# The channel MLP's first layer of an attention, gated-mixer and token/channel-mixer kernel: seven block products in place of eight, tokens in two parts

## The chip, the cores and the metric

One core of one Trainium2 chip runs the kernel. The metric is device time in microseconds (us). TensorE (PE) does the matrix products, VectorE (DVE), ScalarE (ACT) and GpSimd (POOL) the elementwise work, and SyncE (SP) issues the DMAs. Every engine takes its own instructions in a fixed order and waits on the others by semaphores.

## The reference

Three stages in a row, on 4 batches of 448 tokens with 768 channels. All weights come as 64-bit floats.

```python
def _attn_ref(q, k, v, g_q, g_k):            # 12 heads of 64
    q_n, k_n = rmsnorm(q, g_q), rmsnorm(k, g_k)
    attn = softmax(q_n @ k_n.T / sqrt(64))
    return attn @ v

def _moe_ref(x, w_in, w_spatial, b_spatial, w_out):
    h = np.maximum(x @ w_in, 0.0)
    u, v = h[..., :512], h[..., 512:]
    v_n = layernorm(v)
    v_s = np.einsum('ts,bsd->btd', w_spatial, v_n) + b_spatial[None, :, None]
    return (u * v_s) @ w_out

def _moe2_ref(x, w_tok1, w_tok2, w_ch1, w_ch2):
    xt = x.transpose(0, 2, 1)
    h = np.maximum(xt @ w_tok1, 0.0) @ w_tok2
    u = x + h.transpose(0, 2, 1)
    h2 = np.maximum(u @ w_ch1, 0.0) @ w_ch2  # 768 -> 1536 -> 768, the channel MLP
    return u + h2
```

## The kernel before, in words

Nearly every product is done at close to fp32 accuracy with three passes over values split in two (HI, rounded to fp32r, and LO, the rest): HI*HI, HI*LO and LO*HI (PASSES). A split is one ScalarE copy for HI and one subtraction for LO. A weight that comes as 64 bits is first made into an fp32 word by `convert`: one ScalarE Abs, two VectorE tensor_scalar and two VectorE scalar_tensor_tensor.

The program builds a list of operations and does not issue them as it writes them. `Plan.issue` gives each operation a cost and a time to be visible elsewhere (`estimate`), runs a forward and a backward list schedule eight times (`place`), keeps the shortest, and issues every engine's instructions in the order of its start times. The order on each engine is therefore static on the chip, and it follows from those estimates and from the buffers: a pool tag with `bufs` buffers makes its next tile wait for all users of the one that many tiles before. A `fence` opens a new pool where older ones lay, after all their users. PSUM has eight banks, in three kinds ("sc", "tp", "mm"). Nearly all instructions have line 405, where the planned calls are made, so this text goes by tiles.

The stages: attention per pair of heads, merged with the preparation of weights (`prepare_v`, `prepare_uo`, `prepare_next`) and with the gated mixer `moe` of the batches that are done; `moe` of the last batch beside the first steps of the token MLP (`first_tokens`); the token MLP (`Tokens`, tiles h1ps, u_ps); the channel MLP (`channels`, tiles h2ps, o_ps).

In `Tokens`, `sums` leaves u in fp32 tiles x, `store` writes them to the scratch u_d, and `turn` transposes each x tile and splits it into `ut`: 96 transposes on TensorE, 24 copies on ScalarE and 24 subtractions on VectorE of 128x448.

In `channels` (pools `keep`, `wp`, `cp`) the hidden layer has 12 blocks f of 128, taken in pairs. For each pair and each of four token blocks (512, 512, 512, 256), `up` makes two products of 18 matmuls (6 blocks of channels, 3 passes) into h2ps, with Relu and split out of PSUM, and then `down` of the block before adds its part of the second layer into `acc`: per 128 tokens two halves of 12 matmuls of 384 columns and one VectorE add. The weights of f = 0 and 1 come split from scratch (c1_d, c2_d, made in `prepare_next`); those of the ten others are loaded as 64 bits, converted and split in the stage itself, 40 times 128x384, with the subtraction on GpSimd. The tiles c1 and c2 have three buffers each.

Of the kernel before, what the change touches and what calls it, by code (L numbers as in the profile page):

```python
# [21 lines left out]
HI, LO = 0, 1  # L22
# [127 lines left out]
class Plan:  # L150
# [63 lines left out]
    def estimate(self, engine, fn, out, ins, kwargs):  # L214
# [29 lines left out]
        return max(475, shape[0] * n * 4 / 260), 2000  # L244
# [192 lines left out]
def attention_moe_mixer(  # L437
# [95 lines left out]
    c1_d = [scratch([P, 2, KD, P], F32R, f"c1_d{f}") for f in range(2)]  # L533
    c2_d = [scratch([P, 2, DM], F32R, f"c2_d{f}") for f in range(2)]
# [345 lines left out]
    def prepare_next(mp):  # L880
# [25 lines left out]
        n = NX // P  # L906
        for f in range(2):
            for j in range(0, KD, n):
                piece(
                    wdram(w_ch1)[j * P:(j + n) * P, f * P * W:(f + 1) * P * W].rearrange(  # L910
                        "(j p) f -> p j f", p=P), P, (n, P), c1_d[f][:, :, j:j + n])
                yield
        for f in range(2):
            for t in range(0, DM, NX):
                piece(wdram(w_ch2)[f * P:(f + 1) * P, t * W:(t + NX) * W], P, (NX,), c2_d[f][:, :, t:t + NX])
                yield

# [94 lines left out]
    class Tokens:  # L1012
# [75 lines left out]
        def turn(self, b, n, ut):  # L1088
            for j in range(n * KD // 2, (n + 1) * KD // 2):

                tp = psum.tile([P, C * P], "tp", "tp")
                for c, (t, m) in enumerate(TOK):
                    nc.tensor.transpose(tp[:, t:t + P], self.x[b, c][:, j * P:(j + 1) * P], ident)
                tpf = tp[:, :S]
                bs = slice(b * S, (b + 1) * S)
                nc.scalar.activation(ut[j][:, HI, bs], tpf, AF.Copy)
                nc.vector.tensor_tensor(
                    ut[j][:, LO, bs], tpf, ut[j][:, HI, bs].bitcast(F32), op=ALU.subtract)
                yield

# [5 lines left out]
    def channels(wp, cp, ut):  # L1106
        blocks = [(t0, min(512, NTOK - t0)) for t0 in range(0, NTOK, 512)]
        out_f = out.rearrange("b s d -> (b s) d")
        G = 2
        c1, c2 = {}, {}  # L1110
        N = DM // 2

        def load_up(f):
            t = wp.tile([P, 2, KD, P], F32R, tag="c1", bufs=3, name="c1")
            c1[f] = t
            if f < 2:
                nc.sync.dma_start(out=t.bitcast(F32), in_=c1_d[f].bitcast(F32))
                return
            for i in range(2):
                js = slice(i * KD // 2, (i + 1) * KD // 2)  # L1120
                raw = weights(
                    wp, "s", 2,
                    wdram(w_ch1)[i * N:(i + 1) * N, f * P * W:(f + 1) * P * W].rearrange(
                        "(j p) f -> p j f", p=P),
                    P, (KD // 2, P))
                convert(wp, "word", 1, raw, P, N, t[:, HI, js], t[:, LO, js], (KD // 2, P))

        def load_down(f):
            t = wp.tile([P, 2, DM], F32R, tag="c2", bufs=3, name="c2")
            c2[f] = t  # L1130
            if f < 2:
                nc.sync.dma_start(out=t.bitcast(F32), in_=c2_d[f].bitcast(F32))
                return
            for i in range(2):
                ns = slice(i * N, (i + 1) * N)
                raw = weights(
                    wp, "s", 2, wdram(w_ch2)[f * P:(f + 1) * P, i * N * W:(i + 1) * N * W], P, (N,))
                convert(wp, "word", 1, raw, P, N, t[:, HI, ns], t[:, LO, ns])
# [43 lines left out]
        for f0 in range(0, KC, G):  # L1182
            for nb, blk in enumerate(blocks):
                for f in range(f0, f0 + G):
                    for _ in up(f, blk):
                        pass
# [118 lines left out]
```

## Time and profile before

| | |
|---|---|
| median of 3 runs | 956.19 us (954.49 to 959.67) |
| the profiled execution | 952.84 us |
| its span, first to last instruction | 951.1 us |
| TensorE busy | 915.1 us (96%) |
| VectorE busy | 567.9 us (60%) |
| ScalarE busy | 452.1 us (48%) |
| GpSimd busy | 370.1 us (39%) |
| mean granted TensorE clock | 0.996 |

The busy share is a mean over stages. The channel MLP takes the last 350 us or so. TensorE's matmuls are pipelined: one that the profile gives 337 ns follows its neighbour after about half of that, so the pace of a run of them is read from the chain of work that ended last, which gives a stretch and a count.

### The profile page before, as it was taken

The numbers are of one execution on the slowest core, as the hardware profiler recorded it, in microseconds if no ns is written. First come the engines' busy times: TensorE is split into PE (matmuls) and PEld (weight loads), VectorE is DVE, ScalarE is ACT, GpSimd is POOL, SyncE is SP. The second block draws the span as 40 slices with busy tenths as digits, with TensorE's granted clock in tenths as the row PEclk, the third lists the DMA queues.
The fourth block names the chain that finished last, engine by engine and source line by source line (L and its number), as shares of the span: only waits on it lengthen the run. The fifth ranks groups of instructions, "written<-read, shape, count | busy, mean of one in ns | idle before, by whom it ended". The sixth has DMA issues, their size and how long they took to land.

```text
span 951.1 us, 15484 instructions
## 1 busy us (share of the span) xinstructions
PE 915.1 (96%) x5328; PEld 736.9 (77%) x5328; DVE 567.9 (60%) x1254; ACT 452.1 (48%) x1135; POOL 370.1 (39%) x538
## 2 busy tenths in 40 slices
PE   3898999999999999999999999999999999999998
PEld 1344366668767777677889999899898998999898
DVE  4787878775776767764151367534665556555434
ACT  5887877777676777765342345301312213122100
POOL 3767766785666664654124123101201102011100
PEclk9998999999999999999999999999999999999999
DMA  6544465666534565332673475721211212111024
GB/s 153 138 101 134 116 172 149 158 188 184 163 92 107 172 207 179 97 98 99 220 223 129 142 246 181 266 85 34 78 56 36 64 34 83 50 51 50 17 89 144
DMA packets 124654, 118.58 MB, mean 125 GB/s; under 512 B 74784, under 2 KB 108128, under 8 KB 123040
## 3 DMA queue, kind: packets, MB, share of 16 engines
q1 hardware_dynamic: 124576, 117.59, 41.0%
q8 instruction: 42, 0.69, 0.3%
q14 instruction: 36, 0.29, 0.1%
HBM read 89.77 MB, written 27.79 MB: 124 GB/s over the span
## 4 chain that ended last, share of the span: by engine, by line
PE 82%; ACT 5%; DVE 5%; DMA 3%; issue 2%; POOL 2%; SPq 1%; ACTq 0%; POOLq 0%; DVEq 0%
PE o_ps L405 18%; PE h2ps L405 18%; PE tp L405 9%; PE av L405 6%; PE xps L405 6%; PE ups L405 6%; PE sc L405 6%; PE sps L405 4%; PE u_ps L405 3%; PE h1ps L405 3%; PE vps L405 3%; ACT e L405 2%; DVE nm L405 1%; SPq L405 1%; DMA x<-x_d 1%
## 5 line engine op out<-in xcount | busy, mean ns | idle before, releaser
L405 PE MATMUL o_ps<-c,h 128*128 128x384 f32 x1008 | 179.7, 337 | 0.0
L405 PE MATMUL h2ps<-ut,c 128*128 128x512 f32 (+1 forms) x864 | 178.9, 364 | 0.0
L405 PEld LDWEIGHTS o_ps<-c,h 128*128 128x128 f32 x1008 | 175.0, 188 | 2.0 <-DVE acc L405 0.5
L405 PEld LDWEIGHTS h2ps<-ut,c 128*128 128x128 f32 x864 | 148.1, 189 | 24.3
L405 POOL TENSOR_SCALAR e<-e,sums 112x448 f32<-112x448 f32 x192 | 122.8, 656 | 63.0 <-DVE sums L405 35.1
L405 POOL TENSOR_TENSOR c<-word,c 128x384 fp32r<-128x384 f32 x40 | 40.5, 1014 | 265.1 <-ACT c L405 241.7
L405 ACT ACTIVATE e<-sc,nm 112x448 f32<-112x448 f32 x192 | 120.0, 637 | 29.1 <-PE tp L405 15.0
L405 DVE TENSOR_REDUCE nm<-sc 112x1 f32<-112x448 f32 x192 | 110.0, 614 | 22.3 <-PE sc L405 22.0
L405 PEld LDWEIGHTS tp<-ident,e 112*128 112x128 f32 x672 | 75.3, 142 | 47.0 <-POOL e L405 16.6
L405 PE MATMUL tp<-ident,e 112*128 112x112 f32 x672 | 101.9, 267 | 6.4 <-POOL e L405 3.2
L405 DVE TENSOR_TENSOR acc<-o_ps,acc 128x384 f32<-128x384 f32 x140 | 77.2, 555 | 29.6 <-PE o_ps L405 28.9
L405 ACT ACTIVATE h<-h2ps 128x512 fp32r<-128x512 f32 (+1 forms) x48 | 25.8, 538 | 116.5 <-PE h2ps L405 114.9
L405 ACT ACTIVATE c<-word 128x384 fp32r<-128x384 f32 x40 | 21.0, 525 | 123.0 <-DVE word L405 58.2
L405 DVE SCALAR_TENSOR_TENSOR h<-h2ps,h 128x512 fp32r<-128x512 f32 (+1 forms) x48 | 29.9, 624 | 82.3 <-ACT h L405 82.2
L405 ACT ACTIVATE et<-tp 128x448 f32<-128x448 f32 x120 | 63.4, 544 | 20.5 <-PE tp L405 19.9
L405 PE MATMUL ups<-xp,wu 128*128 128x448 f32 x288 | 69.6, 379 | 1.4 <-ACT vr L405 0.7
L405 PE MATMUL av<-et,v 128*64 128x448 f32 x288 | 67.4, 563 | 0.0
L405 PE MATMUL xps<-wo,g 128*128 128x256 f32 x432 | 63.3, 291 | 0.1
L405 PEld LDWEIGHTS xps<-wo,g 128*128 128x128 f32 x432 | 55.1, 190 | 5.0 <-issue 2.3
L405 PEld LDWEIGHTS ups<-xp,wu 128*128 128x128 f32 x288 | 51.7, 189 | 8.6 <-ACT vr L405 1.1
L405 DVE TENSOR_SCALAR word<-word 128x384 f32<-128x384 f32 (+1 forms) x92 | 34.2, 372 | 37.1 <-ACT word L405 35.7
L405 PE MATMUL vps<-wv,xp 128*128 128x512 f32 x216 | 55.1, 402 | 0.0
(105 smaller groups left out, 1414.5 us busy)
## 6 DMA issues: line engine op xcount, KB each, us to landing
raw<-in_moe_w_ch_dram SPq DMA_DIRECT2D x40, 384.0 KB, 3.2
wu<-wu_d SPq DMA_DIRECT2D x16, 768.0 KB, 5.1
wo<-wo_d SPq DMA_DIRECT2D x12, 1024.0 KB, 5.1
raw<-in_q_dram SPq DMA_DIRECT2D x48, 112.0 KB, 3.0
acc<-u_d SPq DMA_DIRECT2D x14, 384.0 KB, 8.2
out_dram<-o SPq DMA_DIRECT2D x28, 192.0 KB, 1.9
v<-in_v_dram SPq DMA_DIRECT2D x48, 96.0 KB, 2.6
x_d<-xo SPq DMA_DIRECT2D x36, 128.0 KB, 2.4
```

The costliest lines, as they stand in the source:

```text
L405: getattr(getattr(self.nc, op.engine), fn)(*args, **kwargs)
```

## The change

The first channel layer, u times w_ch1, is done by seven products of blocks in place of eight, in the form with sums that are used again. For two hidden blocks f (a pair p), both operands are cut into 2 by 2 blocks: the weights into two f by two halves of the channels (a11, a12, a21, a22), the turned tokens into two halves of the channels by two halves of a part of the tokens (b11 to b22). Four sums on either side and seven sums of the products (`plus`) give the four blocks of the hidden layer. The tokens come in two parts (SPANS): 768, with products of n = 384 columns, and 1024, with n = 512. A product has 9 matmuls (3 blocks of channels, 3 passes), so that a part takes 6 x 7 x 9 matmuls.

What else moves: `turn` goes; `read` loads u back from u_d, transposes it, copies it out of PSUM and makes the seven splits and four sums per block of channels in SBUF. The first part is read during the token stage (pool `stage`), the second while the first part's last `down`s run; the seven `ut` tiles have one buffer each. The weights go through scratch as fp32 words, unsplit, all twelve f: six in the attention stage (`prepare_words`), two beside the last `moe`, four in the channel stage, three pieces a pair. Each part splits them anew: `load_up` seven splits and four sums of 128x384 per pair, `load_down` four splits. All subtractions and sums of these steps are on VectorE. `load_down` has one buffer `word` and the c2 tiles of one pair (bufs=2); `load_up` one w1 and seven c1. `down` adds as before; the last adds are written into acc and stored from there. In `estimate`, a DMA's time to be visible goes from 2000 ns to 2400 ns plus 1.2e-3 ns per byte.

```diff
-        return max(475, shape[0] * n * 4 / 260), 2000
+        size = shape[0] * n * 4
+        return max(475, size / 260), 2400 + 1.2e-3 * size
...
+    def prepare_words(pool, fs, NX, raws, words):
+        def piece(src, dims, dst, n):
+            raw = weights(pool, *raws, src, P, dims)
+            tag, bufs, size = words
+            t = pool.tile([P, size], F32, tag=tag, bufs=bufs, name="part")[:, :n]
+            convert(pool, None, 0, raw, P, n, None, None, at=t.bitcast(U32))
+            nc.sync.dma_start(out=dst, in_=t)
...
+    SOON, KNOWN = 6, 8
+    MORE = 3
+    READ, C1, C2, SUMS = nc.vector, nc.vector, nc.vector, nc.vector
+    IN_MP = NX, ("wraw", 2), ("wpart", 2, 2 * NX)
...
+        def split(self, hi, lo, src, on):
+            nc.scalar.activation(hi, src, AF.Copy)
+            on.tensor_tensor(lo, src, hi.bitcast(F32), op=ALU.subtract)
+
+        def read(self, pool, xs, bufs):
+            n, k = self.n, self.n // P
+            end = self.SPANS[self.s][1]
+            for jj in range(self.KH):
+                halves = []
+                for kh in range(2):
+                    x = pool.tile([P, 2 * k, P], F32, tag="x", bufs=xs, name="x")
+                    c = (kh * self.KH + jj) * P
+                    nc.sync.dma_start(
+                        out=x, in_=u_d[self.t0:end, c:c + P].rearrange("(m p) c -> p m c", p=P))
+                    t = pool.tile([P, 2, n], F32, tag="stage", bufs=bufs, name="stage")
+                    for g in range(2):
+                        tp = psum.tile([P, k, P], "tp", "tp")
+                        for m in range(k):
+                            nc.tensor.transpose(tp[:, m], x[:, g * k + m], ident)
+                        nc.scalar.activation(t[:, g], tp.rearrange("p m c -> p (m c)"), AF.Copy)
+                        yield
+                    halves.append(t)
+                b11, b12, b21, b22 = (t[:, g] for t in halves for g in range(2))
...
+                split(self.B11, b11, READ)
+                split(self.B21, b21, READ)
+                split(self.B22, b22, READ)
+                nc.vector.tensor_tensor(b22, b22, b12, op=ALU.subtract)
+                split(self.T3, b22, READ)
+                nc.vector.tensor_tensor(b12, b12, b11, op=ALU.subtract)
+                split(self.T1, b12, READ)
+                nc.vector.tensor_tensor(b11, b11, b22, op=ALU.add)
+                split(self.T2, b11, READ)
+                nc.vector.tensor_tensor(b21, b21, b11, op=ALU.subtract)
+                split(self.T4, b21, READ)
+                yield
+
+        def load_up(self, p):
+            w = self.wp.tile([P, 2, 2, self.N], F32, tag="w1", bufs=1, name="w1")
+            for r in range(2):
+                nc.sync.dma_start(out=w[:, r], in_=c1_d[2 * p + r])
...
+                self.wp.tile([P, 2, self.N], F32R, tag="c1", bufs=7, name="c1") for _ in range(7)]
...
+        def load_down(self, p):
+            for f in (2 * p, 2 * p + 1):
+                t = self.c2[f] = self.cp.tile([P, 2, DM], F32R, tag="c2", bufs=2, name="c2")
+                for i in range(2):
+                    ns = slice(i * self.N, (i + 1) * self.N)
+                    w = self.cp.tile([P, self.N], F32, tag="word", bufs=1, name="word")
+                    nc.sync.dma_start(out=w, in_=c2_d[f][:, i])
+                    self.split(t[:, HI, ns], t[:, LO, ns], w, C2)
...
+        def up(self, p):
+            n = self.n
+            a11, s2, a12, s3, s1, a22, s4 = self.c1.pop(p)
...
+            v = tile("v")
+            nc.scalar.activation(v, product(a11, self.B11), AF.Copy)
+            u2 = plus(tile("u2"), product(s2, self.T2), v)
+            hidden(0, 0, plus(v, product(a12, self.B21), v))
+            yield
+            u3 = plus(tile("u3"), product(s3, self.T3), u2)
+            p5 = product(s1, self.T1)
+            u4 = plus(u2, p5, u2)
+            c22 = plus(tile("v"), p5, u3)
+            hidden(1, 1, c22)
+            yield
+            hidden(1, 0, plus(u3, product(a22, self.T4), u3))
+            hidden(0, 1, plus(u4, product(s4, self.B22), u4))
+            yield
...
+        def rest(self, cp):
+            self.cp = cp
+            prev = None
+            more = prepare_words(cp, range(KNOWN, KC), self.N, ("x", 3), ("stage", 2, 1024))
+            for s in range(len(self.SPANS)):
+                self.load_acc(s)
+                for p in range(self.PAIRS):
+                    for _ in range(MORE if s == 0 else 0):
+                        next(more, None)
+                    yield from self.up(p)
+                    here, reading = (s, p, self.n), iter(())
+                    if p + 1 < self.PAIRS:
+                        self.load_up(p + 1)
+                    elif s + 1 < len(self.SPANS):
+                        self.begin(s + 1)
+                        self.load_up(0)
+                        reading = self.read(cp, 3, 2)
+                    if prev is not None:
+                        for _ in self.down(*prev):
+                            next(reading, None)
+                            yield
+                    self.load_down(p)
+                    prev = here
...
-        (prepare_next(mp), C + 2 * KT + 4 * XN, UO1 + 0.5, NP - 2),
+        (chain(prepare_next(mp), prepare_words(mp, range(SOON), *IN_MP)), C + 2 * KT + 8 * SOON, UO1 + 0.5, NP - 2),
...
+        (moe(mp, B - 1), MOE, 0, 1), (prepare_words(mp, range(SOON, KNOWN), *IN_MP), 8 * (KNOWN - SOON), 0, 1),
```

## Rows read from the trace of the kernel before

**Rows 1.** The page, busy time and share of each engine

```profile
PE 915.1 (96%) x5328; PEld 736.9 (77%) x5328; DVE 567.9 (60%) x1254; ACT 452.1 (48%) x1135; POOL 370.1 (39%) x538
```

**Rows 2.** Stretches: length; busy us of PE, PEld, DVE, ACT, POOL; clock, DMA

```profile
0.00:190.00 190.00, 159.11 (x876) 88.27 (x877) 143.24 (x339) 145.09 (x393) 128.87 (x208) 0.98 0.52 140
190.00:460.00 270.00, 269.20 (x1744) 196.65 (x1744) 176.12 (x421) 185.78 (x505) 162.71 (x257) 1.00 0.49 146
...
700.00:760.00 60.00, 60.00 (x329) 55.49 (x329) 33.36 (x69) 13.35 (x27) 9.14 (x9) 1.00 0.18 53
```

**Rows 3.** The chain that ended last, from 604 us: start, length, what

```profile
604.46 0.44 PE tp L405 x4
...
639.76 4.32 PE h2ps L405 x36
644.08 8.32 PE o_ps L405 x48
652.41 8.20 PE h2ps L405 x36
...
947.61 0.56 DVE o L405
```

**Rows 4.** Waits from 593 us: waiter <- awaited, us in total, times, longest

```profile
ACT h L405 <- PE h2ps L405: 114.9, 24, 11.8
...
PEld o_ps L405 <- DVE acc L405: 0.5, 3, 0.2
```

**Rows 5.** Groups by shape: out<-in xcount | busy us, mean ns | idle before

```profile
L405 DVE TENSOR_TENSOR acc<-o_ps,acc 128x384 f32<-128x384 f32 x140 | 77.2, 555 | 29.6 <-PE o_ps L405 28.9
...
L405 DVE SCALAR_TENSOR_TENSOR word<-raw,word 128x384 uint32<-128x384 uint32 x80 | 44.2, 552 | 1.2
...
L405 DVE SCALAR_TENSOR_TENSOR h<-h2ps,h 128x512 fp32r<-128x512 f32 x36 | 24.9, 691 | 67.8 <-ACT h L405 67.7
...
L405 ACT ACTIVATE c<-word 128x384 fp32r<-128x384 f32 x40 | 21.0, 525 | 123.0 <-DVE word L405 58.2 <-PE h2ps L405 49.5 <-PE o_ps L405 15.2
...
L405 DVE TENSOR_SCALAR word<-word 128x384 f32<-128x384 f32 x40 | 14.3, 358 | 33.4 <-ACT word L405 33.0
...
L405 DVE TENSOR_TENSOR ut<-tp,ut 128x448 fp32r<-128x448 f32 x24 | 14.3, 617 | 5.2 <-ACT ut L405 5.1
```

**Rows 6.** VectorE in order of time: start, length, operation, count, idle before

```profile
562.56 0.95 DVE L405 TENSOR_TENSOR xh<-x,xh 128x768 fp32r<-128x768 f32 x1
563.43 0.55 DVE L405 TENSOR_TENSOR x<-u_ps,x 128x384 f32<-128x384 f32 x1
...
709.00 0.55 DVE L405 SCALAR_TENSOR_TENSOR word<-raw,word 128x384 uint32<-128x384 uint32 x1
709.47 0.56 DVE L405 TENSOR_TENSOR acc<-o_ps,acc 128x384 f32<-128x384 f32 x1
...
725.45 1.15 DVE L405 SCALAR_TENSOR_TENSOR word<-raw,word 128x384 uint32<-128x384 uint32 x2
```

**Rows 7.** DMA issues: transfer, count, KB each, median us from issue to landing

```profile
raw<-in_moe_w_ch_dram SPq DMA_DIRECT2D x40, 384.0 KB, 3.2
...
acc<-u_d SPq DMA_DIRECT2D x14, 384.0 KB, 8.2
...
x<-x_d SPq DMA_DIRECT2D x12, 384.0 KB, 4.8
u_d<-x SPq DMA_DIRECT2D x12, 384.0 KB, 2.9
...
stage<-in_moe_w_spatial_dram SPq DMA_DIRECT2D x4, 196.0 KB, 2.7
```

**Rows 8.** Tile wpart on VectorE: duration ns min/median/max, first and last start, forms

```profile
L405 DVE TENSOR_SCALAR wpart<-wpart x88: 231/284/3223, 48.0 to 409.5; 128x256 f32<-128x256 f32 x41, 128x256 uint32<-128x256 uint32 x41, 128x192 f32<-128x192 f32 x2, 128x192 uint32<-128x192 uint32 x2
L405 DVE SCALAR_TENSOR_TENSOR wpart<-raw,wpart x88: 345/416/2368, 61.1 to 415.9; 128x256 uint32<-128x256 uint32 x82, 128x192 uint32<-128x192 uint32 x4, 64x256 uint32<-64x256 uint32 x2
```

More of the change, by code (lines that the diff above doesn't have):

```diff
@@ L1103, in store @@
             nc.sync.dma_start(out=u_d[b * S + t:b * S + t + m, :], in_=self.x[b, c][:m])
[L1106 to L1110, printed above, removed]
-        N = DM // 2
[L1113 to L1138, printed above, removed]
-        def up(f, blk):
-            t0, n = blk
-            ps = psum.tile([P, 512], "sc", "h2ps")
-            yield from run(
-                ps[:, :n],
-                [(c1[f][:, w, j], ut[j][:, a, t0:t0 + n]) for j in range(KD) for a, w in PASSES], 100)
-            t = cp.tile([P, 2, 512], F32R, tag="h2", bufs=5, name="h2")
-            nc.scalar.activation(t[:, HI, :n], ps[:, :n], AF.Relu)
-            nc.vector.scalar_tensor_tensor(
-                t[:, LO, :n], ps[:, :n], 0.0, t[:, HI, :n].bitcast(F32), ALU.max, ALU.subtract)
-            hs[f, t0] = t
-        def down(f0, blk):
-            t0, n = blk
-            for m in range(t0 // P, (t0 + n) // P):
-                ms = slice(m * P - t0, m * P - t0 + P)
@@ L1243, in first_tokens @@
         yield from tok.hidden(0, 1)
-    merge((moe(mp, B - 1), MOE, 0, 1), (first_tokens(), 2 + C + 8, 0, 1))
-    keep, wp = successors(
-        [pairs, mp], left, (ctx, "keep", "left"), (ctx, "chan_w", "left"))
-    ut = [keep.tile([P, 2, NTOK], F32R, tag=f"ut{j}", bufs=1, name=f"ut{j}") for j in range(KD)]
+    merge(
+        (moe(mp, B - 1), MOE, 0, 1), (prepare_words(mp, range(SOON, KNOWN), *IN_MP), 8 * (KNOWN - SOON), 0, 1),
+        (first_tokens(), 2 + C + 8, 0, 1))
+    keep, wp, stage = successors(
+        [pairs, mp], left, (ctx, "keep", "left"), (ctx, "chan_w", "left"), (late, "stage", "right"))
+    ch = Channels(keep, wp)
+    ch.begin(0)
+    ch.load_up(0)
     def tokens():
@@ L1257, in tokens @@
                     tok.split(b + 1, c)
-            yield from tok.turn(b, 0, ut)
             if b + 1 < B:
@@ L1265, in tokens @@
                 yield from tok.hidden(b + 1, 1)
-            yield from tok.turn(b, 1, ut)
+            if b == TURNED:
+                reading.append(ch.read(stage, 3, 2))
+    TURNED = (ch.SPANS[0][1] - 1) // S
+    reading = []
     for _ in tokens():
-        pass
-    cp, = successors([tok.p], late, (ctx, "chan", "right"))
-    channels(wp, cp, ut)
+        for steps in reading:
+            next(steps, None)
+    for _ in reading[0]:
+        pass
+    cp, = successors([tok.p, stage], late, (ctx, "chan", "right"))
+    out_f = out.rearrange("b s d -> (b s) d")
+    for _ in ch.rest(cp):
+        pass
     nc.issue(psum)
```

148 lines of the change are left out of this document (87 added, 61 removed).

## The prediction

> **What bounds the kernel now.** I read the page's shares first: TensorE is busy for 915.1 of 951.1 us, no other engine for more than 60% [rows 1]. A mean hides stages, so next the stretches. In the first 190 us TensorE is busy 159.1 us, the place of nearly all its idle time; from 190 to 460 us it is busy 269.2 of 270, and in the channel MLP 60.0 of 60 [rows 2]. The chain that ended last says the same of the channel MLP: it is TensorE alone, h2ps and o_ps in turn, up to the last add [rows 3]. The waits confirm it: ScalarE's Relu waited 114.9 us for h2ps, and TensorE's weight loads waited 0.5 us in all for VectorE [rows 4]. So TensorE's own work is the bound, and what is taken from it is won as long as the others keep up. VectorE is the one to watch: it is busy 33.4 us of 60 in this stage [rows 2].
>
> **TensorE's work.** Its pace comes from the chain, not from the matmuls' durations: 36 of h2ps with 512 columns in 8.20 us (0.228 each), 36 with 256 in 4.32, 48 of o_ps with 384 in 8.32 (0.173) [rows 3]. Before, a pair of hidden blocks costs 3 x 8.20 + 4.32 = 28.9 us, six pairs 173.5. After, a pair has 63 matmuls in each part: 63 x 0.173 = 10.9 us with 384 columns, 63 x 0.228 = 14.4 with 512, together 25.3, six pairs 151.7. That saves 21.8 us. The second layer stays: 1008 matmuls, 12.5 us a pair in the first part (72), 16.7 in the second (96). Transposes go from 96 to 84, 0.11 us each (four in 0.44) [rows 3]: 1.3 us. So TensorE needs **23.1 us less**. Both widths have their pace in the rows, so this term is sure; all else is what TensorE will have to wait.
>
> **VectorE in the first part.** The price of an operation is its pace behind another, below its duration: an add of 384 takes 555 ns [rows 5], but where work is queued the next starts 0.47 us on, and behind a subtraction of 768 in SBUF 0.87 on [rows 6]; between them 512 wide comes to about 0.60, an estimate from those two. Per pair of the first part: 7 `plus`, 4 in `hidden`, 11 in `load_up`, 4 in `load_down`, 12 adds, that is 38 x 0.47 = 17.9 us. Three pieces of words come on top: two tensor_scalar of 358 ns and two scalar_tensor_tensor of 552 each by duration [rows 5], 1.8 us, or 1.6 where other work lies between; I take 1.7 x 3 = 5.1. Together 23.0 us against TensorE's 10.9 + 12.5 = 23.4: VectorE is 98% full, where it was 56%. In the second part it is 11 x 0.60 + 31 x 0.47 = 21.2 against 31.0: roomy.
>
> **The refill of c2.** `load_down` can only write when the `down` before has read c2 to its end (bufs=2 is one pair), and its four pieces share one buffer `word`. A piece costs a landing of 2.7 us (the 196 KB load, near its 192) [rows 7], a ScalarE copy of 0.53 and a subtraction of 0.56 [rows 5], 3.8 in all; the first is there already and needs 1.1. The fourth is in after 1.1 + 3 x 3.8 = 12.5 us, and I allow 0.8 for other work ahead of it on the two engines: 13.3. TensorE's cover in between is the next `up` (10.9) and the first six matmuls of `down`, which need only half (1.0): 11.9. So 1.3 us are missing per pair, while VectorE is nearly full; five gaps give **6.5 us**. Low end 1.5 (0.3 a gap, the two engines free); high end 14, from the rival below.
>
> **The seam of the parts.** After the first part's last `up`, TensorE has `down` of pair 4 (12.5), then waits for c2 of pair 5, then has `down` of pair 5. The second part's products need the seven `ut`, which have one buffer each, so the splits of `read` start behind that `up`: 33 x 0.60 = 19.9 us on VectorE with 24 adds (11.3) and 4 splits beside them, some 33 us in a stretch of 36. In the second wait of 13.3 us lie the first six matmuls (1.0), the transposes of two of the three blocks (32 x 0.11 = 3.5) and perhaps one product (2.1): **6 us** of TensorE idle. Low end 3, if the planner puts pair 4's `down` ahead of part of that `up`; high end 9, without the product and with VectorE late. In the old kernel nothing of this exists; its weights had three buffers.
>
> **The start.** The first part's tokens are complete after batch 1. A store of 2.9 us and a load of 4.8 [rows 7] come before the first transposes, and then 33 x 0.47 = 15.5 us of VectorE beside some 8 of the token MLP: 31 us. TensorE has about as much left: seven half steps of 22 matmuls at 0.173 and 36 transposes, 30.7. What `turn` did on VectorE (24 at 617 ns [rows 5]) falls away. I take **2 us**, 0 to 5.
>
> **The end.** The gap for the last c2 has no next `up`, only what was kept of the last one. Each `up` of the second part is 14.4 us and a gap needs 12 to 13, so the order can carry 1 to 2 us on from gap to gap: over four gaps most of what the last needs. **1.5 us**, 0 to 6.
>
> **The attention stage.** Twelve pieces of 256 with split are replaced by 24 of 256 and 24 of 128 without. At the medians of 284 and 416 ns [rows 8] a piece of 256 is 1.4 us of VectorE, one of 128 about 0.9 (an estimate: half the width of the same four): 12 x 1.4 + 24 x 0.9 = 37 us more, into 190 to 460 us, where VectorE is busy 176 of 270 and TensorE has next to no gap [rows 2]. GpSimd loses 12 subtractions. That the work fits is no proof that it hides: single conversions took up to 3.2 us [rows 8], and the first 190 us show what 75% on VectorE can look like [rows 2]. On the other side, landings counted at 2.4 to 2.9 us are closer to the rows (2.7 to 4.8 [rows 7]) than 2.0 was, and a better order could win something in the first 190 us. **+1 us**, -5 to +8. Sixteen pieces beside the last `moe` fall on a VectorE with room and cost nothing.
>
> **Sum.** -23.1 + 6.5 + 6 + 2 + 1.5 + 1 = -6.1 us. The span of 951.1 becomes 945.0. The profiled execution has 952.84 us, 1.7 around its span, and the median of 956.19 lies 3.4 above that; I keep both: 945.0 + 5.1 = **950 us**. Its own range, with half of each end, is 942 to 958.
>
> **The rivals.**
>
> *The others keep up.* The order fills the gaps with work from elsewhere, and only the low ends remain (1.5 + 3): 956.2 - 23.1 + 4.5 = 937.6. For it speaks how densely the old order packs TensorE [rows 3]; against it, that there the others were half idle.
>
> *VectorE sets the pace of the first part (the slower side).* Dependent operations follow each other at 0.60 us, longer than the duration: two conversions in 1.15 [rows 6]. If the 38 operations of a pair, chains of sums and splits, come at 0.555, a pair costs 38 x 0.555 + 3 x 1.82 = 26.6 us against 23.4, 3.2 more, 19 in six pairs. At the seam 33 at 691 ns (the 512-wide one [rows 5]) and 28 at 0.555 are 38.3 against TensorE's 30.3: 8 more. With the 4.5 of start, end and attention: 956.2 - 23.1 + 31.5 = 965. It decides from (23.4 - 5.1) / 38 = 0.48 us per operation, hardly above the 0.47 of the rows; half of it makes the high end of 14 above. The Trainium skill speaks for it: "VectorE: DVE Perf Modes", section "The DRAIN you can't avoid", says that the next operation does not start until the pipe has emptied. By that rule the time would be that of this rival. The rows where an add starts before the operation ahead of it has ended disagree, for operations that don't depend on each other [rows 6].
>
> *The refill takes longer.* With 3.2 us of landing (384 KB [rows 7]), or as much in waits on SP, where stores and loads stand in one line, a gap grows by 1.5 us: 5 x 1.5 + 1.5 at the seam on top of the forecast, 959. A burst of loads landed in 8.2 us [rows 7], which shows that it can.
>
> *The words press on the attention stage.* Its term becomes +8: 957.
>
> That the change doesn't cut TensorE's work can't be: the counts and both widths are fixed.
>
> **How the numbers follow.** Forecast 0.40, the others keep up 0.18, VectorE's pace 0.18, the refill 0.12, the words 0.12. About 0.5% (4.8 us) is what a measurement of this kernel tells from no change, so faster is below 951.4 and slower above 961.0. Of the forecast 0.25 is faster and 0.15 same; keeping up adds 0.18 to faster, and a better order in the first 190 us 0.02; VectorE's pace 0.18 to slower; refill and words are 0.17 same and 0.05 slower. That is 0.45, 0.32, 0.23. The range 936 to 965 leaves out a third of the first rival, half of the second and a little of the rest, 0.19.
>
> **What would show it.** In the profile after: h2ps at 0.173 and 0.228 us per matmul, 756 of them; TensorE's gaps in the first part just ahead of o_ps, ended by a c2 split; one gap of some 6 us at the seam; VectorE near 95% busy from the first product to the seam and near 70% behind it; 190 to 460 us no longer by more than 2 us. The forecast is wrong if the first part shows no gaps (then 938), if TensorE waits there for `plus` or `hidden` rather than for c2 (then 965), or if the time has moved ahead of the token MLP.

## The result and the profile after

The changed kernel takes 969.87 us (median of four, 966.02 to 971.78), the kernel before 957.45 (954.49 to 959.67): a ratio of 1.0131 (1.0097 to 1.0166), 12.4 us slower. The forecast was 950 us with a range of 936 to 965, so both the sign and the range were wrong. The profiled execution of after has 969.4 us and a span of 967.6, 16.5 above that of before; that execution of before was 4.6 us below the median of its kernel, so some 4 of the 16.5 are that execution's. e13 to e15 below point to the attention stage for them.

The page of after, busy time and share of each engine, beside [rows 1]:

```profile
PE 911.5 (94%) x5208; PEld 730.8 (76%) x5208; DVE 725.5 (75%) x1672; ACT 522.8 (54%) x1297; POOL 326.8 (34%) x486
```

VectorE has 158 us more and GpSimd 43 less, because the sums and subtractions are on VectorE now, and there are more of them. TensorE has 120 instructions fewer (108 products, 12 transposes) but only 3.6 us less of busy time: a run of matmuls that trickles still counts as busy. So the stretches come next, in the columns of [rows 2] (length; PE, PEld, DVE, ACT, POOL; clock, DMA share, GB/s):

```profile
0.00:190.00 190.00, 152.86 (x800) 81.83 (x801) 135.14 (x330) 139.59 (x375) 122.69 (x197) 0.96 0.51 138
190.00:460.00 270.00, 267.65 (x1699) 193.21 (x1701) 204.20 (x548) 188.19 (x520) 156.28 (x245) 1.00 0.56 164
593.00:640.00 47.00, 44.86 (x249) 42.96 (x248) 39.26 (x82) 27.06 (x60) 5.62 (x5) 0.93 0.57 181
640.00:700.00 60.00, 58.30 (x333) 57.47 (x332) 59.89 (x137) 23.11 (x47) 0.00 (x0) 1.00 0.65 205
700.00:760.00 60.00, 58.34 (x339) 56.97 (x338) 55.71 (x118) 28.42 (x56) 0.00 (x0) 1.00 0.46 135
745.00:795.00 50.00, 45.56 (x232) 38.83 (x231) 46.59 (x88) 29.21 (x54) 0.00 (x0) 0.97 0.48 155
```

The first 190 us hold 800 matmuls and transposes where they held 876, the next 270 hold 1699 where they held 1744. The time is lost in front. Where each stage ends is read from the start of the last matmul of a tile, in one profiled execution: the unsplit scores `whole`, the values `av`, the mixer's `xps`, the token MLP's `u_ps`, and `o_ps`.

| stretch, up to the last | before, us | after, us | longer by |
|---|---|---|---|
| whole | 117.9 | 131.4 | 13.5 |
| av (end of the attention stage) | 460.6 | 477.6 | 3.5 |
| xps (last mixer) | 537.5 | 557.4 | 2.9 |
| u_ps (token MLP) | 598.5 | 617.0 | -1.4 |
| o_ps (channel MLP) | 947.2 | 963.8 | -1.9 |

The lines behind the second row, before and after:

```profile
L405 PE MATMUL av<-et,vrest x96: 539/539/591, 40.6 to 460.6; 128*64 128x448 f32 x96
```

```profile
L406 PE MATMUL av<-et,vrest x96: 539/539/591, 41.7 to 477.6; 128*64 128x448 f32 x96
```

The 2.9 us of the last mixer are work that moved forward: 85 matmuls of h1ps, the token MLP's first product, lie between the last av and the last xps where 67 did, and 18 of them at 0.174 us are 3.1 us.

The attention stage is 17.0 us longer, 13.5 of it by 131 us. The words of the change can't have done these 13.5 by their work, because they had not begun: tile `part` on VectorE (columns of [rows 8]) has its first operation at 263.9 us.

```profile
L406 DVE TENSOR_SCALAR part<-part x160: 210/293/1235, 263.9 to 722.0; 128x256 f32<-128x256 f32 x32, 128x256 uint32<-128x256 uint32 x32, 128x128 f32<-128x128 f32 x32, 128x128 uint32<-128x128 uint32 x32
```

What TensorE waited for up to 132 us (awaited tile, total, times, longest), first before, then after:

```profile
PE tp L405 <- POOL raw L405: 12.9, 1, 12.9
...
PE tp L405 <- POOL e L405: 3.2, 9, 0.7
```

```profile
PE tp L406 <- POOL e L406: 13.1, 17, 2.2
PE tp L406 <- POOL raw L406: 10.7, 1, 10.7
PE sc L406 <- ACT whole L406: 4.9, 2, 4.3
```

The same transposes of the softmax's `e` wait 13.1 us for GpSimd instead of 3.2. No operation of that stretch was edited: other operations stand ahead of them in the fixed order, which differs on TensorE from the 24th matmul or transpose on. So the question for the experiments was what had changed that order: the new landing times, or the 48 pieces of words in the list.

For the stages behind, a loss is counted: the length of a stretch less its matmuls and transposes at their pace. The chain of after (start, length, what):

```profile
599.41 1.76 PE h1ps L406 x10
601.17 1.73 PE u_ps L406 x10
...
622.65 0.56 DVE ut L406
623.82 9.24 PE h2ps L406 x36
633.42 6.25 PE h2ps L406 x36
...
655.51 4.66 PE h2ps L406 x24
660.17 2.09 PE o_ps L406 x12
662.26 1.39 PE h2ps L406 x8
664.35 0.70 PE o_ps L406 x4
...
786.23 8.04 PE h2ps L406 x27
...
796.18 12.29 PE h2ps L406 x54
```

The paces are those of the prediction: 36 of 384 columns in 6.25 us are 0.174 each, 54 of 512 in 12.29 are 0.228. By them TensorE lost 6.1 us from the last `xps` to 617.3 (0.5 before), 5.9 from there to 640 (start), 2.5 from 640 to 745 (first part), 8.1 from 745 to 795 (seam) and 0.3 behind that: 22.9 in all. (The 2 to 3 us that a low clock adds, last section, are in the start and the seam.) The lines of 655 to 664 us show why the first part is so dense: the order doesn't run `up` and `down` one after the other, it mixes them in runs of 4 to 24 matmuls.

### The profile page after: what moved, and what is told of

The parts are those of the page before. It is cut to its first block, busy times and chain, and to the rows that moved or that the text cites. A ratio compares the mean times of both kernels' runs of the same rounds, so it can differ in the third digit from the quotient of the medians.

```text
span 967.6 us, 16228 instructions
## 1 busy us (share of the span) xinstructions
PE 911.5 (94%) x5208; PEld 730.8 (76%) x5208; DVE 725.5 (75%) x1672; ACT 522.8 (54%) x1297; POOL 326.8 (34%) x486
## 4 chain that ended last, share of the span: by engine, by line
PE 73%; DVE 9%; ACT 7%; DMA 4%; issue 3%; POOL 2%; SPq 1%; ACTq 0%; DVEq 0%; POOLq 0%
PE o_ps L406 17%; PE h2ps L406 14%; PE tp L406 8%; PE av L406 6%; PE ups L406 5%; PE vps L406 5%; PE sc L406 5%; PE xps L406 4%; PE sps L406 3%; ACT e L406 3%; PE u_ps L406 2%; PE h1ps L406 2%; DVE nm L406 2%; POOL e L406 2%; DMA x_d<-xo 1%
## 5 line engine op out<-in xcount | busy, mean ns | idle before, releaser
L406 PE MATMUL o_ps<-c,h 128*128 128x384 f32 x1008 | 188.0, 336 | 1.7 <-DVE acc L406 1.7
L406 PE MATMUL h2ps<-ut,c 128*128 128x384 f32 (+1 forms) x756 | 172.1, 373 | 6.1 <-ACT ut L406 2.9
L406 PEld LDWEIGHTS h2ps<-ut,c 128*128 128x128 f32 x756 | 140.1, 193 | 25.0 <-ACT ut L406 4.7
L406 PE MATMUL tp<-ident,e 112*128 112x112 f32 x672 | 105.2, 272 | 17.7 <-POOL e L406 13.6
L406 DVE TENSOR_TENSOR acc<-o_ps,acc 128x384 f32<-128x384 f32 x168 | 89.6, 555 | 30.1 <-PE o_ps L406 29.7
L406 ACT ACTIVATE c<-word 128x384 fp32r<-128x384 f32 x48 | 24.9, 518 | 92.5 <-PE o_ps L406 76.3
L406 DVE SCALAR_TENSOR_TENSOR part<-raw,part 128x256 uint32<-128x256 uint32 (+2 forms) x160 | 68.1, 438 | 1.2
L406 ACT ACTIVATE c<-w 128x384 fp32r<-128x384 f32 x84 | 42.9, 521 | 48.0 <-DVE w L406 20.6
L406 DVE TENSOR_SCALAR part<-part 128x256 f32<-128x256 f32 (+5 forms) x160 | 47.3, 312 | 28.2 <-ACT part L406 25.5
L406 PE MATMUL sc<-kt,qt 64*112 64x448 f32 x384 | 52.3, 387 | 0.4 <-ACT e L406 0.2
```

Of the source, the lines that this page charges most:

```text
L406: getattr(getattr(self.nc, op.engine), fn)(*args, **kwargs)
```

## The experiments

Two theories for the attention stage: **the landing times** (the new estimate redraws the order) and **the words** (their pieces press there), the second in two forms, by their work on the chip or by their place in the list from which the order is drawn. For the channel MLP: **the refill** of c2 against **VectorE's chain** in `read`. All runs, with the end of the first scores, of the attention stage, of the token MLP and of the channel MLP. The stage times are those of one profiled execution; each ratio is against runs of before from the same session. Where one run is all there is, a few us count for little: in those sessions runs of before went from 954.24 to 962.23 us.

| kernel | median us | ratio (95%) | whole | av | u_ps | o_ps |
|---|---|---|---|---|---|---|
| before | 957.45 | | 117.9 | 460.6 | 598.5 | 947.2 |
| after | 969.87 | 1.0131 (1.0097 to 1.0166) | 131.4 | 477.6 | 617.0 | 963.8 |
| e1 | 960.83 | 1.0029 (1.0003 to 1.0055) | 124.2 | 467.0 | 603.6 | 952.6 |
| e2 | 970.96 | 1.0132 (1.0102 to 1.0163) | 124.2 | 490.7 | 624.7 | 967.7 |
| e3 | 951.64 | one run | 124.0 | 465.7 | 599.6 | 946.0 |
| e4 | 964.33 | one run | 122.7 | 473.4 | 609.4 | 958.3 |
| e5 | 966.5 | one run | 133.6 | 478.6 | 617.0 | 960.9 |
| e6 | 968.79 | 1.0106 (1.0056 to 1.0156) | 118.6 | 469.7 | 614.0 | 964.7 |
| e7 | 985.65 | one run | 117.5 | 483.7 | 625.3 | 980.1 |
| e8 | 986.5 | one run | 126.5 | 471.4 | 618.0 | 980.9 |
| e9 | 958.42 | 1.0006 (0.9989 to 1.0024) | 120.5 | 471.4 | 605.8 | 952.1 |
| e10 | 964.1 | 1.0061 (1.0038 to 1.0084) | 127.7 | 474.0 | 607.7 | 958.6 |
| e11 | 962.31 | 1.0050 (1.0026 to 1.0074) | 122.2 | 467.8 | 603.6 | 955.7 |
| e12 | 962.06 | one run | 128.0 | 481.3 | 618.1 | 956.5 |
| e13 | 982.91 | 1.0255 (1.0234 to 1.0276) | 121.1 | 473.8 | 633.3 | 978.8 |
| e14 | 963.98 | 1.0059 (1.0041 to 1.0078) | 118.8 | 470.9 | 608.7 | 956.7 |
| e15 | 947.89 | 0.9885 (0.9868 to 0.9901) | 122.0 | 466.7 | 599.4 | 944.3 |
| e16 | 960.22 | one run | 117.5 | 477.4 | 615.1 | 954.7 |
| e17 | 972.02 | 1.0140 (1.0110 to 1.0170) | 125.9 | 478.9 | 614.2 | 968.4 |

### The landing times: e1, e2, e4

e1 is before with the new estimate, e2 after with the old one, e4 before with a flat 2400 ns.

```diff
-        return max(475, shape[0] * n * 4 / 260), 2000
+        size = shape[0] * n * 4
+        return max(475, size / 260), 2400 + 1.2e-3 * size
```

> The kernel before with the new landing times in the planner's estimate (2400 ns plus 1.2e-3 per byte in place of 2000 ns), nothing else. In the changed kernel the last unsplit scores (tile whole) ended at 131.4 us against 117.9, and the last values product (vrest) at 477.6 against 460.6. Theory 1, the landing estimate made that order: this kernel shows both delays, 131 and 476, and about 970 us. Theory 2, the added words and the rest of the changed program made it: 118, 461 and 957 us. Theory 3, every change of estimates or program draws another order and the length of the attention stage scatters by many us: anything from 115 to 132 and 952 to 972.

> The changed kernel with the old landing estimate of 2000 ns. Theory 1 (estimate): the attention stage is as before, scores to 118 us, values to 461, and the time falls by 13 to 17 us to 953 to 957. Theory 2 (words and program): 131, 477 and 970 us. Theory 3 (scatter): in between or beyond.

> The kernel before with a flat 2400 ns as landing estimate, 0.08 to 1.2 us a transfer away from the estimate of the first run. If a better or worse landing time is what counts (theory 1), the scores end within 3 us of the first run. If the order is a draw (theory 3), they end more than 4 us apart.

The attention stage ends 6.4 us later in e1 and 12.8 in e4, though neither issues one operation more or less than before: only a number in the estimate differs. So an order drawn anew can cost several us by itself. How many is less sure than these two ends say: executions of one order differ by up to 6 us at a like place (e13 to e15 below), e1's median is only 2.8 us above that of before, and e4's one run 6.3. And the new landing times aren't the cause in after: with the old ones (e2) the stage ends at 490.7, later still.

### The words: e3 and e5

In e3 the 48 pieces of f below 6 are not in the list at all; the 16 of f = 6 and 7 still are, and the planner moves them from beside the last mixer into the attention stage (their first VectorE operation is at 329.7 us). In e5 the 48 are in the list, but their instructions (`skip`) aren't issued. In the traces TensorE, VectorE, ScalarE and GpSimd then run the operations of after in the order of after, the words aside, from the first to the last.

```diff
-        (chain(prepare_next(mp), prepare_words(mp, range(SOON), *IN_MP)), C + 2 * KT + 8 * SOON, UO1 + 0.5, NP - 2),
+        (chain(prepare_next(mp), iter(())), C + 2 * KT, UO1 + 0.5, NP - 2),
```

```diff
+            if op.skip:
+                continue
```

> The changed kernel without the 48 pieces of words in the attention stage (the pairs of f below 6 read the words of f = 6 and 7, so that part of the weights' conversion is left out). Theory 1: no earlier than 470 us for the last values product, time about 968. Theory 2, the words press on VectorE and SP there: 461 and about 955. Theory 3: neither number is bound to come.

> The changed kernel, planned as it is and with its order on every engine, but the 48 pieces of words of the attention stage are not issued (their conversion is left out; the pairs of f below 6 read the words of f = 6 and 7). Without them in the plan the last values product ended at 465.7 us, with them at 477.6. If the words' own work on VectorE, ScalarE and the queue delays the rest (theory A), this run ends it at 465 to 468 us. If the other order that the plan takes because of them is the cause (theory B), it stays at 474 to 478, and the last unsplit scores, which end before the first word is loaded, stay at 131.

This pair decides for after. Without the 48 pieces in the list the stage ends at 465.7 us, with e1's first stretch (the same order up to some 270 us). With them in the list it ends at 478.6, as in after, and neither ScalarE nor VectorE has run an operation of a word by then: the first one on `part` comes at 483.0 us on VectorE, for the 16 pieces of f = 6 and 7.

```profile
L411 PE MATMUL av<-et,vrest x96: 539/539/590, 43.0 to 478.6; 128*64 128x448 f32 x96
L411 DVE TENSOR_SCALAR part<-part x64: 214/348/1235, 483.0 to 720.4; 128x384 f32<-128x384 f32 x16, 128x384 uint32<-128x384 uint32 x16, 128x256 f32<-128x256 f32 x8, 128x256 uint32<-128x256 uint32 x8
```

The waits of e5 up to 132 us are those of after, not those of before:

```profile
PE tp L411 <- POOL raw L411: 10.8, 1, 10.8
PE tp L411 <- POOL e L411: 10.1, 14, 2.2
PE sc L411 <- ACT whole L411: 4.7, 2, 4.2
```

So the words cost in after by the order that was drawn with them, from the first microseconds on, and hardly by their own time on VectorE. What that time is worth can be read too: from the same TensorE instruction, at 263 us where the first word begins, to the last av after takes 214.4 us and e5 212.6, 1.8 us for the work of 47 pieces, as far as one execution of each can show. This holds for the order of after. In e2, e7 and e16 the loss lies mostly behind the first scores, and no such run was made for them.

### The words elsewhere, and other draws: e6, e8, e9, e10, e11

e6 lists 32 of the 48 pieces beside the last `moe` (SOON = 2), e8 is e6 with the old estimate; e9, e10 and e11 list 32 pieces in the attention stage, 24 beside the last `moe`, four a pair in the first part, with estimates of 2000, 2400 and 2200 ns. Where a piece is listed is not where it runs, since the planner may place it earlier. Counted by ScalarE's first operation on `part`, 34 pieces run in e6 before the last av, 32 in e8, 38 or 39 in e9 to e11 and 47 in after.

```diff
-    SOON, KNOWN = 6, 8
-    MORE = 3
+    SOON, KNOWN = 4, 7
+    MORE = 4
```

> The changed kernel with the words of f = 2 to 7 prepared beside the last mixer stage and only f = 0 and 1 in the attention stage (SOON = 2). Theory A (the words' work where VectorE is full): the attention stage ends near 468, the mixer stage grows by at most 3 us, VectorE having some 50 us of idle time there, and the time is 956 to 960. Theory B (any such order is a draw): the attention stage is anywhere from 461 to 480.

> As the run with the words beside the mixer, with the old landing estimate of 2000 ns. If the old estimate gives the better order once the words are away (it did for the kernel before, 460.6 against 467.0 us to the last values product), the time is 950 to 955; if the order is a draw, it can be on either side of the other run's by 5 us or more.

> The changed kernel with another division of the words (f = 0 to 3 in the attention stage, 4 to 6 beside the last mixer, 7 to 11 in the channel MLP, four pieces a pair) and the old landing estimate of 2000 ns. It was chosen because its plan ends the attention stage early. If the order of the attention stage is what cost the changed kernel its time, the last values product comes at 462 to 468 us and the time is 948 to 955, below the kernel before. If any plan with these words loses there, 474 us or later and 962 or more. Twenty pieces of words in the first part in place of 16 make VectorE fuller there: a loss of up to 5 us in the channel MLP.

> The same division of the words with a flat landing estimate of 2400 ns: another draw of the order. Order theory: the attention stage ends within a few us of where its plan has it, 462 to 470, time 949 to 957. If the landing estimate itself has an effect, this run is 6 us or more behind the one with 2000 ns.

> The same with 2200 ns, a third draw: 462 to 470 us for the last values product, 948 to 957 us in all. If the landing estimate has a steady effect, it lies between the other two; if orders are draws, it need not.

e6 wins 7.9 us at the end of the attention stage and gives 4.9 of them back by the end of the token MLP; its interval overlaps that of after. e8 loses 12.2 us more than e6 behind the token MLP. e9 is level with before, the best of the versions that do all the work, though its forecast was 948 to 955; e10 and e11 differ from it in one number and are 0.6 and 0.4% slower.

Over all kernels here the stage ends later the more pieces of words run in it, and in a group of three or more the ends scatter by 11 to 13 us:

| pieces before the last av | kernels | av, us | mean |
|---|---|---|---|
| none | before, e1, e4 | 460.6 to 473.4 | 467.0 |
| 16 | e3, e15 | 465.7, 466.7 | 466.2 |
| 32 to 39 | e6, e8 to e11, e13, e14, e17 | 467.8 to 478.9 | 472.2 |
| 43 to 49 | after, e2, e7, e12, e16 | 477.4 to 490.7 | 482.1 |
| 47 planned as in after, none issued | e5 | 478.6 | |

So it doesn't look like chance alone: orders drawn with more pieces end later. e5 shows for one such order that the pieces needn't run for that. Why the planner's orders get worse with them isn't shown.

### The order held: e13, e14, e15

To part order from work, e13 to e15 take the priorities that before's own plan gave to the operations of the attention stage, spread the words between, and place once more (estimate 2000 ns). e13 lists the words as after does, e14 as e9 does, and e15 leaves out the 48, as e3 does. The lines are those of e13; the two numbers differ from run to run.

```diff
+        for i, op in enumerate(ops):
+            n = seen[op.key] = seen.get(op.key, -1) + 1
+            if op.key == 'word':
+                weight.append(-724435 + 233669 * n / words)
+                continue
+            own = best[3][i] + shift
+            weight.append(pinned[op.key][n] if n < len(pinned.get(op.key, ())) else own)
...
+            nc.filling = pool is mp
```

> The changed kernel with its own division of the words and the old landing estimate, planned once more with the priorities that the plan of the kernel before gave to the operations of the attention stage; the words are put in between by their turn. If the free order is what cost the attention stage its time, the last unsplit scores end at 118 us as before and the last values product at 461 to 468, against 477.6 in the changed kernel and 490.7 with its own plan at 2000 ns. If the words' work itself presses there, 472 or later. Time: 955 to 965, since its channel MLP has one pass of planning only.

> The same priorities with f = 0 to 3 in the attention stage, 4 to 6 beside the last mixer and 7 to 11 in the channel MLP. Values to 461 to 468 us; with the 3 to 10 us that the channel MLP has won in the draws so far, 948 to 956 us in all, below the kernel before. If it is 958 or more, the change wins nothing even at a good order of the attention stage.

> The same priorities, and the 48 pieces of words of f below 6 left out (their pairs read the words of f = 6 and 7): the block products alone, with the attention stage as before. Values to 460 to 462 us. The forecast for all but the attention stage was 7 us less than before: 948 to 952. If the three waits (start, first part, seam) cost what they did in the changed kernel, 21 us of the 23, 954 to 957.

The first stretch is back at 118.8 to 122.0. The order was held up to the first word: in the traces of before and of these three the four engines run the same operations in the same order up to 318 us. So their differences up to there are those of executions. At one TensorE instruction in this stretch (the 1600th) before is at 304.2 us, e14 at 306.2, e13 at 308.2 and e15 at 310.3. That is a scatter of 6 us, with before's profiled execution at its early end; e15's end at 466.7 against 460.6 is no more than that.

The last line of the edit makes the three runs other than meant: it counts every piece made in the pool `mp` as a word to be spread, those beside the last mixer too. Operations on `part` up to the last av (length; VectorE, ScalarE; clock, DMA) in e13, e14 and e15:

```profile
0.00:473.80 473.80, 43.78 (x144) 12.86 (x36) 0.99 0.52 149
```

```profile
0.00:470.90 470.90, 40.69 (x142) 12.62 (x36) 0.99 0.52 148
```

```profile
0.00:466.70 466.70, 21.79 (x64) 6.11 (x16) 0.99 0.49 138
```

So e13 and e14 have 36 pieces in the stage, not 48 and 32, and e15 has 16. From the 1600th instruction to the last av before takes 156.4 us, e15 156.4, e14 164.7 and e13 165.5: 8 to 9 us for 20 pieces more. By the forecast of e13 an end at 473.8 speaks for the words' own work. But from the first word on the order is another one too, and these runs don't part the two. The windows of e14 and of e15 show the place (columns as in the section on the result):

```profile
360.00:420.00 60.00, 55.95 (x340) 38.45 (x342) 48.22 (x141) 38.99 (x110) 27.07 (x43) 1.00 0.54 156
```

```profile
360.00:420.00 60.00, 59.05 (x374) 41.65 (x373) 45.62 (x122) 41.61 (x114) 28.89 (x45) 1.00 0.42 116
```

TensorE gets through 340 instead of 374 instructions there. From the last av to the end of the token MLP e13 takes 21.7 us more than e14. 26 of its pieces run between the last av and the last xps, and the chain from 544 to 569 us goes through four loads of words (14.6 us) and the operations on `part` between them. e15 is 1.15% faster than before: the seven products, without those 48 pieces, are worth 10.3 us. That is no version to keep, since the 48 pieces are needed. With them no order here beat before: e14's forecast named 958 or more as the sign of it, and e14 took 963.98. How much of the words' cost a better order could hide isn't settled.

### The channel MLP: e7, e12, e16, e17

e12 leaves out the four sums of `read`. e16 gives `word` two buffers and x two. e17 is e9 with two of the four sums on GpSimd, e7 is after with all weight splits on GpSimd.

```diff
-                nc.vector.tensor_tensor(b22, b22, b12, op=ALU.subtract)
...
-                nc.vector.tensor_tensor(b12, b12, b11, op=ALU.subtract)
...
-                nc.vector.tensor_tensor(b11, b11, b22, op=ALU.add)
...
-                nc.vector.tensor_tensor(b21, b21, b11, op=ALU.subtract)
```

> The changed kernel with the four sums per block of channels in read left out (12 operations of VectorE per part, and the chains through them; the second layer then gets other values). In the changed kernel TensorE lost some 12 us from the last mixer product to 640 us and some 8 us at the seam of the two parts. If VectorE's chain in read is what it waits for in both places, the first loss falls to 6 to 8 us and the second to 2 to 4. If the refill of c2 is what it waits for at the seam, as forecast, the second stays at 6 to 8.

```diff
-                    w = self.cp.tile([P, self.N], F32, tag="word", bufs=1, name="word")
+                    w = self.cp.tile([P, self.N], F32, tag="word", bufs=2, name="word")
...
-                        reading = self.read(cp, 3, 2)
+                        reading = self.read(cp, 2, 2)
```

> The changed kernel with two buffers for load_down's word (and two in place of three for x in the channel stage, to make room). In the changed kernel TensorE lost 2.5 us in the first part (640 to 745 us) and 8.1 at the seam. If the refill of c2 is what it waits for, as forecast, a gap's refill shortens by some 5 us (two landings beside other work) and both losses fall, the seam's to 4 us or less. If VectorE's chain in read is what it waits for at the seam, its loss stays at 6 to 9.

```diff
-                nc.vector.tensor_tensor(b12, b12, b11, op=ALU.subtract)
+                nc.gpsimd.tensor_tensor(b12, b12, b11, op=ALU.subtract)
...
-                nc.vector.tensor_tensor(b21, b21, b11, op=ALU.subtract)
+                nc.gpsimd.tensor_tensor(b21, b21, b11, op=ALU.subtract)
```

> The first draw with other words (958.4 us, level with the kernel before), with two of the four sums per block of channels in read on GpSimd, which is idle in the channel MLP. Without any sums the seam lost nothing. If the count of VectorE's operations sets the seam, its loss falls from 5.9 to 3 to 5 us and the time is 954 to 959 at an equal attention stage; if the chain through the sums sets it, GpSimd's longer operations make it longer, 7 to 10 us. The attention stage is a new draw, which can move the total by 6 us either way.

```diff
-    READ, C1, C2, SUMS = nc.vector, nc.vector, nc.vector, nc.vector
+    READ, C1, C2, SUMS = nc.vector, nc.gpsimd, nc.gpsimd, nc.vector
```

> The changed kernel with the weights' subtractions of load_up and load_down (15 per pair) on GpSimd in place of VectorE. In the first part VectorE is busy 59.9 of 60 us from 640 to 700. If VectorE's pace is what TensorE waits for in the channel MLP, the first part loses 3 to 6 us of its gaps, the stretch from the token MLP's last product to the last o_ps falls from 347.5 to 341 to 344 us. If the refill of c2 is what it waits for, it stays or grows by 2 to 5 us, since a subtraction on GpSimd took 1014 ns against 552.

Windows of e12, then of e16, where after had TensorE busy 45.56 of 50 us:

```profile
730.00:790.00 60.00, 60.00 (x338) 56.08 (x337) 54.66 (x107) 35.77 (x71) 0.00 (x0) 1.00 0.51 160
```

```profile
745.00:795.00 50.00, 47.50 (x239) 40.23 (x238) 47.53 (x88) 27.98 (x52) 0.00 (x0) 1.00 0.59 187
```

Twelve operations fewer on VectorE per part and the seam's loss falls from 8.1 to 0.1 us. Two buffers `word` bring it to 4.6 and the first part's 2.5 to nothing. With half of the sums on GpSimd (e17), VectorE has fewer operations and the seam still loses some 9.6 us, against 5.9 in e9: that is what was forecast for the chain, not for the count. So the chain of `read` carries the seam, and the refill has a share. e9, e10, e13, e14 and e15 scatter from 5.6 to 8.9 there, and e5, with the order of after, lost some 6.6; so e16's 3.5 us is no sharp figure. At the start the sums matter less: from the last xps to 640 us e12 lost some 10 us, after 12.0, where 6 to 8 had been forecast if VectorE's chain set that too.

GpSimd is no relief: a sum took 1.29 us there against 0.68 on VectorE (medians over both widths), a split of 384 columns 1.02 against 0.55. Lines of e17 and e7:

```profile
L406 POOL TENSOR_TENSOR stage<-stage x12: 1002/1291/1618, 595.1 to 786.3; 128x384 f32<-128x384 f32 x6, 128x512 f32<-128x512 f32 x6
```

```profile
L406 POOL TENSOR_TENSOR c<-w,c x84: 987/1017/2168, 576.1 to 937.9; 128x384 fp32r<-128x384 f32 x84
```

e17 is 13.6 us slower than e9 and e7 16 slower than after, but 7.5 and 6.1 us of that were there at the last av, from another order of the attention stage. From the last u_ps to the last o_ps they take 7.9 and 8.0 us more. (e7 moves 11 subtractions a pair; the 15 of its forecast count the sums too, which stayed.)

## Why the prediction was wrong, point by point

- **The step that failed: the attention stage, +1.** It measured +17.0, of which 2 to 6 us may be before's early execution. The step priced the words as VectorE work and asked whether that work hides; it took the order around it as given, and let a redrawn order only win ("a better order could win something"). What it priced it priced well for this order: the work of the words is worth 1.8 us (e5 against after). What it left out is the order: that of the whole program is drawn anew from a list with 48 pieces more, and e5 has the delay without one of their instructions. The bound of +8 came from the words' work, so it couldn't hold this. The rival "the words press on the attention stage" had the place right, and for after the mechanism and the price wrong. The sign named in the forecast, that the time has moved ahead of the token MLP, is what came.
- **TensorE's work, -23.1.** Right: 756 of h2ps at 0.174 and 0.228 us, 120 instructions fewer. From the last `av` to the last `o_ps`, though, only 0.4 us of the 23.1 are left (+2.9 -1.4 -1.9); the waits below took the rest.
- **The start, +2.** Too small: 5.9 us from 617.3 to 640, and another 5.6 in the token MLP ahead of it. In the chain the first products follow the splits `ut`, and then the clock is low (below). What made the 5.6 in the token MLP stays open; the whole loss there was 6.1 in after, 1.4 in e15 and some 8 in e16. Nor is the 5.9 sharp: e5, with the same order, lost some 3 at the start.
- **The words beside the last mixer, nothing.** Right as far as seen: the 2.9 us of that stretch are the 18 matmuls of h1ps that moved there.
- **The first part, +6.5.** Smaller: 2.5. `down` and `up` are mixed, so a refill of c2 has more to hide behind than the one `up` that I counted, and a `word` landed in 2.4 us rather than 2.7. That the refill was the cause fits e16, where a second `word` buffer leaves no loss. My sum for VectorE, 98% full, was near: 59.89 us of 60 busy up to 700 us, 55.71 of the next 60.
- **VectorE's pace (rival, 965).** It didn't come. VectorE in order of time (start, length, operation, count), in the full stretch:

```profile
654.84 0.55 DVE L406 SCALAR_TENSOR_TENSOR part<-raw,part 128x384 uint32<-128x384 uint32 x1
655.31 0.55 DVE L406 TENSOR_TENSOR w<-w 128x384 f32<-128x384 f32 x1
655.78 0.55 DVE L406 TENSOR_TENSOR c<-w,c 128x384 fp32r<-128x384 f32 x1
656.25 0.55 DVE L406 SCALAR_TENSOR_TENSOR part<-raw,part 128x384 uint32<-128x384 uint32 x1
```

  A start every 0.47 us, below the 0.55 that each takes. The order puts operations of several chains side by side, and that fits [rows 6], where two conversions in a row came 0.60 apart; no run tested it alone. The Trainium skill, "VectorE: DVE Perf Modes", section "The DRAIN you can't avoid", says that the next operation waits for the pipe to empty, and adds that one which is not held starts earlier. These rows start earlier, and the rival took the wait for all.
- **The seam, +6.** Size inside its bounds (8.1 of 3 to 9), cause half right: VectorE's chain in `read` first (e12, e17), the refill second (e16).
- **The end, +1.5.** 0.3: the last refill is covered.
- **The sum.** -23.1 + 17.0 + 5.6 + 5.9 + 2.5 + 8.1 + 0.3, less the 0.7 that the old channel MLP lost itself, is +15.6, against 16.5 measured; the 0.9 between them are not placed. Of the 22.6 us between the -6.1 of the forecast and that, 16 are the attention stage; the start and the token MLP ahead of it add 9.5 and the seam 2.1, the first part and the end take 5.2 off.

## What to carry to other kernels

Where one planner orders the whole program, an edit that adds operations anywhere, or changes one number of its estimates, redraws every stage: bound that term by what redrawn orders did (here 460.6 to 490.7 us for the end of one stage, later with more operations listed in it), not by the work that was added. Where a kernel was kept because its order came out well, the first draw of its successor may lose that part; how before was found is not on record here. To learn what an edit is worth by itself, keep the operations in the list and don't issue them, and compare from the same instruction on. Count in the trace where the added operations ran, since a label in the source doesn't say, and take two executions of one order as the measure of chance: here they differed by up to 6 us within a stage.

## What the runs showed of the hardware

**The clock after a gap.** Windows of after around the start and the seam, columns as above:

```profile
618.00:624.00 6.00, 3.86 (x16) 2.38 (x16) 6.00 (x13) 3.86 (x8) 0.57 (x1) 0.91 0.35 106
624.00:633.00 9.00, 9.00 (x37) 9.00 (x38) 5.21 (x12) 2.50 (x6) 0.00 (x0) 0.68 0.54 183
633.00:640.00 7.00, 7.00 (x42) 7.00 (x41) 7.00 (x17) 4.35 (x10) 0.00 (x0) 1.00 0.84 268
780.00:786.00 6.00, 4.64 (x16) 2.31 (x14) 6.00 (x11) 3.66 (x7) 0.00 (x0) 1.00 0.79 264
786.00:795.00 9.00, 8.78 (x33) 7.24 (x34) 8.47 (x17) 4.58 (x9) 0.00 (x0) 0.81 0.07 21
```

After some 6 us with 16 matmuls and transposes, the granted clock fell to 0.68 in the 9 us behind (part of them at 1.2 GHz, the rest at 2.4), and 36 products of 384 columns took 9.24 us instead of 6.25; at the seam 27 of 512 took 8.04 instead of 6.15. A gap there costs about its own length and 2 to 3 us more, which no term of the sum had.

**Landings.** One of the 64-bit loads for the words beside the last mixer took 7.39 us to land (chain of after), where the loads of its two sizes have medians of 2.9 and 3.0 us, and ScalarE waited up to 4.7 us for one of them:

```profile
539.33 7.39 DMA raw<-in_moe_w_ch_dram
```
